# One list-scheduled order over all engines for a conditioned sliding-window attention and gMLP block

## Chip, cores, metric

The kernel runs on one core of a Trainium2 chip, written instruction by instruction in Bass. The metric is device time in microseconds (us), the median of several executions. A run counts as slow when it is over 1.5% above the fastest run of the same kernel; ratios use the other runs alone. Engines are called PE (TensorE matmul), PEld (its weight load), DVE (VectorE), ACT (ScalarE), POOL (GpSimd) and SP (SyncE, which here only issues DMAs).

## The reference, cut to what matters

```python
S, D, H, Dh, W = 2048, 448, 16, 28, 256        # tokens, width, heads, head width, window
mod = silu(c) @ w_mod                          # six vectors of 448: sa, ca, ga, sb, cb, gb
h = layernorm(x) * (1 + ca) + sa
q, k, v = split(h @ wqkv)                      # 16 heads of 28
p = softmax(where(0 <= i - j < 256, q @ k.T * 28**-0.5, -1e9))
x = x + ga * ((p @ v) @ wo)
h = layernorm(x) * (1 + cb) + sb
z = gelu(h @ w_in)                             # 2048 x 1792
z1, z2 = z[:, :896], layernorm(z[:, 896:])
g = w_sp @ z2 + b_sp                           # spatial matmul, 2048 x 2048 times 2048 x 896
x = x + gb * ((z1 * g) @ w_out)
```

Tokens are worked in 16 tiles of 128. With the window of 256 a tile of queries sees at most three tiles of keys, so attention is 128 "units" (16 tiles times 8 pairs of heads). A unit is six small score products, one exponential over 128 x 768, a mask, and six small products of probabilities with V ("PV").

## The kernel before

The author fixes the order on every engine by the order of the Python calls. The stages follow one another: loads, LayerNorm and QKV of all four blocks of 512 tokens, attention, z2 and z1, spatial matmul and output. Only the projections of the tile before are woven into attention, at fixed units.

```python
    ln1_dve(0) ... ln1_dve(3)
    transp_block(0)
    for tb in range(NB4):                       # QKV of all four blocks
        if tb + 1 < NB4:
            transp_block(tb + 1)
        qkv_block(tb)
        ...
    all_qk = [QKT_ready[k] for k in QKT_ready]  # every score waits for all of QKV
    # ... cut ...
    LAG = 3
    for u in range(LAG, NU + LAG):              # attention: one unit a step
        if u < NU:
            issue_S(u)                          # six score products
            issue_exp_mask(u)                   # ACT exp, DVE multiply with the mask
        issue_PV(u - LAG)
        # ... cut ...
        if tprev >= 0:                          # the tile before, at fixed units
            if ui == 1:   c1(tprev)             # PE transposes o, DVE copies it back
            elif ui == 3: c3(tprev, ...)        # projection with wo, residual
            elif ui == 4: c5(tprev)             # LayerNorm statistics
            elif ui == 7: c6(tprev, ...)        # PE transposes, DVE modulates
```

After attention, the second gate is multiplied into `w_out` on POOL, and the z2 tiles begin:

```python
    t_wout_g = sc.op("pool", lambda e: e.tensor_tensor(
        w_out_g[:], w_out_g[:], gg_sb[:, 1:2, :].broadcast_to([128, 7, D]), ALU.mult), [t_wout, t_gg])
    # ... cut: z2_tile: 8 matmuls, gelu to f32, statistics, normalisation to bf16
```

The softmax here doesn't subtract the row's maximum and nothing guards it: scores larger than these inputs give would overflow.

Of the kernel before, what the change touches and what calls it, by code (L numbers as in the profile page):

```python
# [8 lines left out]
ENGS = ("pe", "act", "dve", "pool", "sp")  # L9


class _Sched:

    def __init__(self, sems):
        self.sems = sems
        self.prog = {e: [] for e in ENGS}
        self.cnt = {e: 0 for e in ENGS}
        self.waited = {e: {} for e in ENGS}
        self.dma_cnt = {}

    def wait(self, eng, tk):
        if tk is None:
            return
        key, val = tk
        if self.waited[eng].get(key, 0) >= val:
            return
        self.waited[eng][key] = val
        self.prog[eng].append(("wait", key, val))

    def op(self, eng, fn, waits=(), sig=True):  # L30
        for w in waits:
            self.waitany(eng, w)
        if sig:
            self.cnt[eng] += 1
            self.prog[eng].append(("op", fn, eng, 1))
            return (eng, self.cnt[eng])
        self.prog[eng].append(("op", fn, None, 0))
        return None

    def waitany(self, eng, w):  # L40
        if w is None:
            return
        if isinstance(w, list):
            for t in w:
                self.waitany(eng, t)
            return
        self.wait(eng, w)

    def dma(self, fn, sem, waits=(), eng="sp"):
        for w in waits:  # L50
            self.waitany(eng, w)
        self.dma_cnt[sem] = self.dma_cnt.get(sem, 0) + 16
        self.prog[eng].append(("op", fn, ("dma", sem), 16))
        return (("dma", sem), self.dma_cnt[sem])

    def emit(self, eng, e):
        for item in self.prog[eng]:
            if item[0] == "wait":
                _, key, val = item
                sem = self.sems[key] if isinstance(key, str) else key[1]  # L60
                e.wait_ge(sem, val)
            else:
                _, fn, key, inc = item
                inst = fn(e)
                if key is not None:
                    sem = self.sems[key] if isinstance(key, str) else key[1]
                    inst.then_inc(sem, inc)


def bass_adaLN_cond__sliding_block__mixer_gmlp__prompt_kernel(  # L70
# [16 lines left out]
    DC = 4  # L87
    CH = 112
    NB4 = NT // 4
# [3 lines left out]
    ARENA_BYTES = 207 * 1024  # L93
    arena = nc.alloc_sbuf_tensor("arena", [128, ARENA_BYTES // 2], BF16)
    base = nc.lookup_mloc(arena).addr
    cursor = [0]

    def alloc(name, shape, dt, at=None):
        size = 1
        for s_ in shape[1:]:  # L100
            size *= s_
        nbytes = (size * mybir.dt.size(dt) + 31) // 32 * 32
        if at is None:
            off = cursor[0]
            cursor[0] += nbytes
        else:
            off = at
        assert off + nbytes <= ARENA_BYTES, (name, off, nbytes)
        return nc.alloc_sbuf_tensor_at(name, list(shape), dt, offset=base + off), off, nbytes

    x_sb, x_off, _ = alloc("x_sb", [128, NT, D], BF16)
    x1 = x_sb
    hT, _, _ = alloc("hT", [CH, DC, S], BF16)
    w_spT, _, _ = alloc("w_spT", [128, NT, S], BF16)
    bsp_bc, _, _ = alloc("bsp_bc", [128, S], BF16)
    modT_sb, _, _ = alloc("modT_sb", [128, 16], F32)
    ident, _, _ = alloc("ident", [128, 128], BF16)
    st_all, _, _ = alloc("st_all", [128, 3, NT, 2, 6], F32)
    mv_all, _, _ = alloc("mv_all", [128, 3, NT, 2], F32)
    ve_all, _, _ = alloc("ve_all", [128, 3, NT], F32)  # L120
    rs_all, _, _ = alloc("rs_all", [128, 3, NT], F32)
    neghalf, _, _ = alloc("neghalf", [128, NT], F32)
    rec_all, _, _ = alloc("rec_all", [128, NT, H], F32)
    mask01, _, _ = alloc("mask01", [128, 2, 128], BF16)
    phase_base = cursor[0]
    xn_all, _, _ = alloc("xn_all", [128, NT, D], BF16)
    wqkv_st, _, _ = alloc("wqkv_st", [CH, DC, 3 * D], BF16)
    WQK, _, _ = alloc("WQK", [CH, DC, 32, 32], BF16)
    wo_g, _, _ = alloc("wo_g", [CH, DC, D], BF16)
    gg_sb, _, _ = alloc("gg_sb", [128, 2, D], F32)  # L130
    sc_sb, _, _ = alloc("sc_sb", [CH, DC], BF16)
    cT_sb, _, _ = alloc("cT_sb", [CH, DC], BF16)
    Vaug, _, _ = alloc("Vaug", [128, NT, H, 32], BF16)
    oT_sb, ot_off, _ = alloc("oT_sb", [CH, 2, DC, 128], BF16)
    o_sb, _, _ = alloc("o_sb", [128, 3, D], BF16)
    NPT = 6
    PT, pt_off, _ = alloc("PT", [128, NPT, 6, 128], BF16)
    xn2, xn2_off, _ = alloc("xn2", [128, 3, D], BF16)
    sc_rep, _, _ = alloc("sc_rep", [CH, DC, 128], BF16, at=xn2_off + 1152)
    identf, _, _ = alloc("identf", [128, 128], F32, at=xn2_off + 2176)  # L140
    qkt_off = cursor[0]
    QKT, _, _ = alloc("QKT", [128, 8, S], BF16)
    abc_end = cursor[0]
    wmodA_sb, _, _ = alloc("wmodA_sb", [CH, DC, 2 * D], BF16, at=qkt_off)
    wmodB_sb, _, _ = alloc("wmodB_sb", [CH, DC, 4 * D], BF16, at=ot_off)
    assert ot_off + DC * 4 * D * 2 <= xn2_off + 1152

    def wm(v):
        return (wmodA_sb, v * D) if v < 2 else (wmodB_sb, (v - 2) * D)
    cursor[0] = phase_base  # L150
    w_in_sb, _, _ = alloc("w_in_sb", [CH, DC, 2 * FH], BF16)
    w_out_g, _, _ = alloc("w_out_g", [128, 7, D], BF16)
    assert cursor[0] <= phase_base + NT * D * 2 + DC * 3 * D * 2
    z2, _, _ = alloc("z2", [128, NT, FH], BF16)
    z1T, _, _ = alloc("z1T", [128, 7, S], BF16)
    z2raw, _, _ = alloc("z2raw", [128, 2, FH], F32)
    tmpg, _, _ = alloc("tmpg", [128, 2, 512], BF16)
    fin, _, _ = alloc("fin", [128, 4, D], BF16)
    d_end = cursor[0]
    assert max(abc_end, d_end) <= ARENA_BYTES, (abc_end, d_end)  # L160

    ps = nc.alloc_psum_tensor("ps", [128, 8, 512], F32)

    sem_names = ["pe", "act", "dve", "pool", "sp"]
    dma_sem_names = ["d_c", "d_wmodA", "d_wmodB", "d_x0", "d_x1", "d_x2", "d_x3", "d_wqkv", "d_wo",
                     "d_win", "d_wout", "d_bsp", "d_wsp0", "d_wsp1", "d_o0", "d_o1", "d_o2", "d_o3"]
    sem_handles = {}
    sem_ctx = []
    for n in sem_names + dma_sem_names:
        cm = nc.semaphore(n)  # L170
        sem_ctx.append(cm)
        sem_handles[n] = cm.__enter__()
    sc = _Sched({k: sem_handles[k] for k in sem_names})
    DS = {k: sem_handles[k] for k in dma_sem_names}
# [3 lines left out]
    wqkv_d = A_wqkv.rearrange("(c p) n -> p c n", p=CH)  # L178
    wo_d = A_wo.rearrange("(c p) n -> p c n", p=CH)
    win_d = B_w_in.rearrange("(c p) n -> p c n", p=CH)  # L180
    wout_d = B_w_out.rearrange("(f p) n -> p f n", p=128)
    wmod_d = w_mod.rearrange("(c p) n -> p c n", p=CH)
    cT_d = c[0].rearrange("(c p) -> p c", p=CH)
    bsp_d = B_b_sp[:].partition_broadcast(128)

    def _dma_c(e):
        with nc.allow_non_contiguous_dma(reason="tiny transposed load of c"):
            return e.dma_start(cT_sb[:], cT_d)
    t_x = [None] * 4
    t_x[0] = sc.dma(lambda e: e.dma_start(x_sb[:, 0:4, :], x_d[:, 0:4, :]), DS["d_x0"])  # L190
    t_c = sc.dma(_dma_c, DS["d_c"])
    t_wmodA = sc.dma(lambda e: e.dma_start(wmodA_sb[:], wmod_d[:, :, 0:2 * D]), DS["d_wmodA"], eng="act")
    t_wqkv = sc.dma(lambda e: e.dma_start(wqkv_st[:], wqkv_d), DS["d_wqkv"])
    for i in range(1, 4):
        t_x[i] = sc.dma(lambda e, i=i: e.dma_start(x_sb[:, 4 * i:4 * i + 4, :], x_d[:, 4 * i:4 * i + 4, :]), DS["d_x%d" % i])
    t_wmodB = sc.dma(lambda e: e.dma_start(wmodB_sb[:], wmod_d[:, :, 2 * D:6 * D]), DS["d_wmodB"], eng="act")
    t_wo = sc.dma(lambda e: e.dma_start(wo_g[:], wo_d), DS["d_wo"])
    t_bsp = sc.dma(lambda e: e.dma_start(bsp_bc[:], bsp_d), DS["d_bsp"])
    for tk in [t_c, t_wmodA, t_wqkv, t_wmodB, t_wo, t_bsp] + t_x:
        sc.wait("sp", tk)  # L200
    t_wspT = []
    for si in range(NT):
        sem = DS["d_wsp%d" % (si % 2)]
        tk = sc.dma(lambda e, si=si: e.dma_start_transpose(out=w_spT[:, si, :], in_=B_w_sp[:, si * 128:(si + 1) * 128]), sem)
        sc.wait("sp", tk)
        t_wspT.append(tk)
# [19 lines left out]

    bank_free = {b: [] for b in range(8)}
    MODV = (0, 1, 3, 4)
    last = None
    t_modT_pe = {}  # L230
    def modT_mm(vis, bank):
        nonlocal last
# [114 lines left out]
    for tb in range(NB4):  # L347
        if tb + 1 < NB4:
            transp_block(tb + 1)
# [368 lines left out]
```

## Time and profile before

| | before |
|---|---|
| median of the first three runs | 435.22 us (432.95 to 438.85) |
| profiled span | 436.2 us |
| PE busy | 359.3 us (82%) |
| DVE busy | 220.0 us (50%) |
| mean granted PE clock | 0.797 |

A window table gives, for each stretch of time, its length and the busy time of PE, PEld, DVE, ACT and POOL in us with instruction counts in brackets; then the granted PE clock (1.00 is full speed), the DMA share, and GB/s. The stretches here are the stages of the kernel before: start, QKV, attention, z2/z1, spatial matmul and output.

```profile
0.00:42.00 42.00, 18.71 (x111) 11.16 (x112) 20.48 (x59) 11.84 (x18) 8.57 (x18) 0.98 0.82 198
42.00:84.00 42.00, 40.26 (x222) 19.50 (x220) 9.40 (x16) 21.10 (x35) 3.60 (x1) 0.89 0.57 129
84.00:238.00 154.00, 125.58 (x1612) 74.97 (x1612) 113.86 (x304) 91.93 (x128) 9.77 (x17) 0.51 0.10 24
238.00:313.00 75.00, 56.97 (x256) 25.70 (x257) 46.87 (x97) 30.74 (x44) 15.53 (x19) 0.88 0.00 1
313.00:436.00 123.00, 117.73 (x551) 54.69 (x559) 29.35 (x44) 0.64 (x2) 32.29 (x28) 1.00 0.05 16
```

Attention takes 154 of 436 us, with no engine full (PE 82%, DVE 74%, ACT 60%, POOL 6%) and the clock at half. The spatial matmul, by contrast, is PE at 96% and full clock. There is little to win there.

Two parts of the page agree. The first line is the chain that ended last, by engine; the others are groups (busy us, mean ns of one, and the idle time before them with its main releaser).

```profile
PE 29%; DVE 26%; issue 24%; POOL 12%; ACT 5%; DMA 3%; POOLq 0%; SPq 0%; DVEq 0%
...
L412 ACT ACTIVATE PT<-ps 128x768 bf16<-128x768 f32 (+2 forms) x128 | 92.2, 771 | 61.7 <-PE ps L401 61.4
...
L419 DVE TENSOR_TENSOR PT<-PT,mask_61 128x512 bf16<-128x512 bf16 x112 | 44.8, 421 | 18.1 <-ACT PT L412 18.1
...
L476 PE MATMUL ps<-wo_g,oT_sb 112*128 112x448 bf16 x64 | 26.5, 570 | 4.0 <-DVE oT_sb L466 4.0
```

The chain is shared between PE and DVE, the mark of two engines handing work to and fro. The masks alone are 44.8 us of DVE. The projection's matmuls take 570 ns each at the granted clock of 0.51 of this stage, where the same width takes 352 ns at 1.00 (the output matmuls of the last stage). The waits of PE (us in total, times, longest):

```profile
PE ps L497 <- DVE xn_73 L488: 23.8, 16, 7.5
PE ps L240 <- ACT sc_sb L224: 15.6, 1, 15.6
PE ps L443 <- DVE o_sb L451: 12.8, 15, 1.4
```

L497 is the transpose of the normalised tile, L443 the first PV product of a tile. Both wait once per tile on something in DVE's in-order queue. The 15.6 us are the conditioning vector at the start. The longest wait, 7.5 us, lies where attention ends. The timeline shows it (start, duration, what, and in brackets the idle time before it):

```profile
238.18 6.15 POOL L539 TENSOR_TENSOR w_out_g<-w_out_g,gg_sb 128x3136 bf16<-128x3136 bf16 x1
238.25 6.21 DVE L488 TENSOR_SCALAR xn_73<-x_sb,mv_all,rs_all 128x448 bf16<-128x448 bf16 x1 [0.65 <-POOL rs_all L276]
```

A normalisation that otherwise takes 0.40 us (395 ns at the least, 396 at the median of the sixteen) takes 6.21 us beside a POOL multiply of 6.15 us, and the two end within 0.2 us of each other (244.33 and 244.46 us). So much the trace shows; that the one held up the other is the author's reading.

### The profile page before, as it was taken

Reading aid. Unit: us, or ns where it says so; the run is one execution under the profiler, and the core shown is the slowest. Engines: PE = TensorE matmul, PEld = TensorE weight load, DVE = VectorE, ACT = ScalarE, POOL = GpSimd, SP = SyncE. Lnnn points to the kernel's source line nnn. Section 1 sums busy time; section 2 is a strip of 40 time slices with the busy share of each in tenths; the row PEclk is TensorE's granted clock in tenths of the full one; section 3 lists DMA queues with packets and bytes.
Section 4 is the critical chain, followed back from the end, with each engine's and each line's share of the span. In section 5 each row is a group of like instructions: output and inputs, shape, how many; then the busy total and the mean of one; then the engine's idle time right before and its main releaser. Section 6 shows DMA issues by size and latency. Waiting matters only on the chain.

```text
span 436.2 us, 6559 instructions
## 1 busy us (share of the span) xinstructions
PE 359.3 (82%) x2749; PEld 186.0 (43%) x2760; DVE 220.0 (50%) x519; ACT 156.3 (36%) x224; POOL 69.8 (16%) x82
## 2 busy tenths in 40 slices
PE   0278999977888888888785567888999999999995
PEld 0243544444555544555453223333444444444442
DVE  0477122467777777777777767775012312313212
ACT  1063464756566655666653222447500000000000
POOL 4010300000000020000002411111033233233231
PEclk9998699955555555555555588999999999999999
DMA  8966646730000043000000000000000100100001
GB/s 211 297 169 102 143 99 145 123 71 2 2 2 2 2 127 97 2 2 2 2 0 2 0 1 2 1 2 0 0 2 0 44 0 0 44 0 11 32 0 44
DMA packets 40638, 19.44 MB, mean 45 GB/s; under 512 B 34176, under 2 KB 39184, under 8 KB 40608
## 3 DMA queue, kind: packets, MB, share of 16 engines
q1 hardware_dynamic: 39232, 14.19, 14.0%
q10 hardware_dynamic: 928, 2.41, 2.1%
q0 software_dynamic: 448, 2.41, 1.9%
q8 instruction: 22, 0.36, 0.4%
q14 instruction: 8, 0.07, 0.0%
HBM read 8.78 MB, written 1.84 MB: 24 GB/s over the span
## 4 chain that ended last, share of the span: by engine, by line
PE 29%; DVE 26%; issue 24%; POOL 12%; ACT 5%; DMA 3%; POOLq 0%; SPq 0%; DVEq 0%
DVE st_all L270 7%; POOL z1T L634 7%; PE ps L401 6%; PE ps L476 6%; POOL rs_all L276 5%; DVE PT L419 5%; PE ps L315 4%; PE ps L443 4%; ACT PT L412 3%; DMA cT_sb<-in_c_dram 3%; DVE xn_73 L488 3%; PE ps L328 3%; DVE z_81 L566 2%; DVE o_sb L451 2%; DVE mv_all L272 2%
## 5 line engine op out<-in xcount | busy, mean ns | idle before, releaser
L412 ACT ACTIVATE PT<-ps 128x768 bf16<-128x768 f32 (+2 forms) x128 | 92.2, 771 | 61.7 <-PE ps L401 61.4
L627 PE MATMUL ps<-w_spT,z_81 128*128 128x512 bf16 x437 | 96.4, 379 | 0.6
L627 PEld LDWEIGHTS ps<-w_spT,z_81 128*128 128x128 bf16 x448 | 43.9, 98 | 52.6
L631 DVE TENSOR_TENSOR tmpg<-ps,bsp_bc 128x512 bf16<-128x512 f32 x28 | 19.4, 692 | 88.7 <-PE ps L627 88.7
L276 POOL TENSOR_TENSOR rs_all<-ve_all,neghalf 128x1 f32<-128x1 f32 (+1 forms) x36 | 21.4, 595 | 251.6 <-DVE ve_all L275 251.6
L401 PE MATMUL ps<-QKT 32*128 32x128 bf16 x720 | 60.4, 297 | 0.9 <-ACT PT L412 0.7
L419 DVE TENSOR_TENSOR PT<-PT,mask_61 128x512 bf16<-128x512 bf16 x112 | 44.8, 421 | 18.1 <-ACT PT L412 18.1
L443 PE MATMUL ps<-Vaug,PT 128*128 128x32 bf16 x720 | 41.5, 190 | 13.6 <-DVE o_sb L451 12.8
L634 POOL TENSOR_TENSOR z1T<-tmpg,z1T 128x512 bf16<-128x512 bf16 x28 | 32.3, 1153 | 93.5 <-DVE tmpg L631 93.5
L443 PEld LDWEIGHTS ps<-Vaug,PT 128*128 128x128 bf16 x720 | 28.8, 105 | 37.8 <-DVE o_sb L451 16.3
L401 PEld LDWEIGHTS ps<-QKT 32*128 32x128 bf16 x720 | 28.3, 118 | 19.6 <-issue 11.3
L556 PE MATMUL ps<-w_in_sb,hT 112*128 112x448 bf16 x128 | 30.4, 394 | 3.2 <-ACT z2raw L560 3.2
L315 PE MATMUL ps<-hT,WQK 112*128 112x512 bf16 x128 | 29.7, 389 | 1.1 <-ACT QKT L318 1.1
L497 PE MATMUL ps<-ident,xn_73 128*112 128x128 bf16 x64 | 10.8, 324 | 23.8 <-DVE xn_73 L488 23.8
L476 PE MATMUL ps<-wo_g,oT_sb 112*128 112x448 bf16 x64 | 26.5, 570 | 4.0 <-DVE oT_sb L466 4.0
L560 ACT ACTIVATE z2raw<-ps 128x896 f32<-128x896 f32 x16 | 14.7, 917 | 34.1 <-DVE z_81 L566 15.8
L580 PE MATMUL ps<-hT,w_in_sb 112*128 112x512 bf16 x112 | 25.7, 379 | 1.3 <-ACT z1T L583 1.3
L331 DVE CAST Vaug<-ps 128x448 bf16<-128x448 f32 x16 | 9.9, 623 | 28.0 <-PE ps L328 27.3
L647 PE MATMUL ps<-w_out_g,z1T 128*128 128x448 bf16 x112 | 21.8, 352 | 2.1 <-POOL z1T L634 2.1
L318 ACT ACTIVATE QKT<-ps 128x512 bf16<-128x512 f32 x32 | 19.0, 599 | 11.2 <-PE ps L315 11.1
L556 PEld LDWEIGHTS ps<-w_in_sb,hT 112*128 112x128 bf16 x128 | 13.3, 109 | 19.8 <-ACT z2raw L560 6.6
L503 DVE TENSOR_SCALAR hT<-ps,modT_sb 112x128 bf16<-112x128 f32 x64 | 21.7, 401 | 0.0
(61 smaller groups left out, 299.2 us busy)
## 6 DMA issues: line engine op xcount, KB each, us to landing
x_sb<-in_A_x_dram SPq DMA_DIRECT2D x4, 448.0 KB, 15.5
out_dram<-fin SPq DMA_DIRECT2D x16, 112.0 KB, 2.1
wmodB_sb<-in_w_mod_dram ACTq DMA_DIRECT2D x1, 1568.0 KB, 13.7
w_in_sb<-in_B_w_in_dram POOLq DMA_DIRECT2D x1, 1568.0 KB, 8.9
wqkv_st<-in_A_wqkv_dram SPq DMA_DIRECT2D x1, 1176.0 KB, 17.1
wmodA_sb<-in_w_mod_dram ACTq DMA_DIRECT2D x1, 784.0 KB, 7.3
w_out_g<-in_B_w_out_dram POOLq DMA_DIRECT2D x1, 784.0 KB, 11.0
bsp_bc<-in_B_b_sp_dram SPq DMA_DIRECT2D x1, 512.0 KB, 9.5
```

What stands on the lines that cost most here:

```text
L270: tks.append(sc.op("dve", lambda e, t=t, ci=ci, s_ap=s_ap: e.bn_stats(st_all[:, slot, t, ci, :], s_ap), src_waits(t)))
L276: t_rs = sc.op("pool", lambda e: e.tensor_tensor(rs_all[:, slot, t0:t1], ve_all[:, slot, t0:t1], neghalf[:, t0:t1], ALU.pow), [t_ve, t_nh])
L315: last = sc.op("pe", lambda e, g=g, kc=kc, bank=bank: e.matmul(ps[:, bank, :], lhsT=WQK[:, kc, 4 * g:4 * g + 4, :].rearrange("p a b -> p ( ...
L401: last = sc.op("pe", lambda e, hh=hh, kb=kb, bank=bank, bi=bi, hg=hg, j=j: e.matmul(ps[:, bank, bi * 128:(bi + 1) * 128], lhsT=QKT[32 * hh ...
L412: t_exp = sc.op("act", lambda e: e.activation(PT[:, pb, :, :].rearrange("p (h b) q -> p h b q", b=3)[:, :, 0:nb, :], ps[:, 2 * sb:2 * sb + ...
L419: t_m = sc.op("dve", lambda e: e.tensor_tensor(ptv[:, :, 0:3:2, :], ptv[:, :, 0:3:2, :], mask01[:].unsqueeze(1).broadcast_to([128, 2, 2, 1 ...
L443: last = sc.op("pe", lambda e, slot=slot, kb=kb, h=h, bi=bi, nb=nb: e.matmul(ps[:, 4, 32 * h:32 * h + 32], lhsT=PT[:, pb, slot, :], rhs=Va ...
L476: last = sc.op("pe", lambda e, cc=cc, tb2=tb2: e.matmul(ps[:, 6, 0:D], lhsT=oT_sb[:, tb2, cc, :], rhs=wo_g[:, cc, :], start=(cc == 0), sto ...
L556: last = sc.op("pe", lambda e, t=t, hf=hf, kc=kc, banks=banks: e.matmul(ps[:, banks[hf], 0:D], lhsT=hT[:, kc, t * 128:(t + 1) * 128], rhs= ...
L580: last = sc.op("pe", lambda e, ft=ft, tb=tb, kc=kc, bank=bank: e.matmul(ps[:, bank, :], lhsT=w_in_sb[:, kc, ft * 128:(ft + 1) * 128], rhs= ...
L627: last = sc.op("pe", lambda e, si=si, ft=ft, tb=tb, bank=bank: e.matmul(ps[:, bank, :], lhsT=z2[:, si, ft * 128:(ft + 1) * 128], rhs=w_spT ...
L634: t_u = sc.op("pool", lambda e, mb=mb, ft=ft, tb=tb: e.tensor_tensor(z1T[:, ft, tb * 512:(tb + 1) * 512], tmpg[:, mb, :], z1T[:, ft, tb * ...
```

## The change

The whole kernel is rebuilt around a small planner. Each operation is declared with its dependencies, its buffer, a priority, and a modelled cost on each engine that could run it. A list scheduler picks, engine by engine, the operation that can start first (ties by priority) and so fixes one order for all five engines. Stages now overlap: block 0's attention can start when block 0's QKV is there, and QKV of blocks 1 to 3 is mixed into it. Loads are issued in the order in which they are needed. Beside that, work moves:

- masks leave DVE for two POOL selects of 256 columns per unit;
- both per-tile PE transposes become DMA transposes issued by SP, on the same queue as the 32 transposes of the spatial weight;
- the second LayerNorm's scale and shift are folded into `w_in` (scale on the rows, shift as a bias row), and the gates' products move to DVE;
- the gelu products leave POOL for DVE, and the z2 buffer becomes bf16.

```diff
-    all_qk = [QKT_ready[k] for k in QKT_ready]
-                w = (S_free[sb] + all_qk) if first else []
+            deps = [QK_op[(hg, j // 4)]] + [QK_op[(4 + hg, kb // 4)] for kb in kbs]
+            s_op = P.op("S%d_%d" % (j, ui), pr, [("pe", 36 * 2 * nb, s_fn)], deps, alloc=ten)
 ...
-            t_m = sc.op("dve", lambda e: e.tensor_tensor(
-                ptv[:, :, 0:3:2, :], ptv[:, :, 0:3:2, :], mask01[:]...broadcast_to([128, 2, 2, 128]), ALU.mult), ...)
+            k_op = P.op("M%d_%d" % (j, ui), pr, [("pool", (2 if nb == 3 else 1) * pool_ns(256), m_pool)],
+                        [e_op] + t_mask, uses=[pt])
 ...
-    c1: four PE transposes of o_sb into PSUM, one DVE copy to oT_sb
+        t1 = P.op("oT%d" % j, pr, [("sp", 100, lambda e, ...: e.dma_start_transpose(
+            out=oT[:, oTt.slot, :, :], in_=o_sb[:, ot.slot, :]))], [nrm, t_opad], alloc=oTt,
+            table="tr", dma=(131072, 2000), uses=[ot])
 ...
+    for n, si in enumerate([6, 7, 8, 9, 10, 11, 0, 1, 2, 3, 4, 5, 12, 13, 14, 15]):
+        for hf in range(2):                     # the spatial weight, 32 transposes, also on SP
+            wsp_op[(si, hf)] = P.op("wsp%d_%d" % (si, hf), 50 + n, [("sp", 100, fn)], deps,
+                                    table="wsp", dma=(300000, 1500))
 ...
+    P.predicted = P.schedule()
+    P.emit(handles, dma_sems)
```

Lines of the diff that name `c1` in words stand for code that was cut.

## The prediction

> **What bounds the kernel now.** The window table gives four stages. Until 42 us it waits for data: the conditioning vector lands at 15.2 us (chain of waits). QKV runs 42 to 84 us. Attention runs to 238 us, 10.14 us per token tile of eight two-head units. The MLP's z2/z1 run to 313 us: 6 us are lost to a Pool multiply of 6.15 us that also stretched a VectorE normalisation to 6.21 us (timeline), then 2.97 us per z2 tile, set by VectorE's statistics chain. The spatial matmul and output end at 436 us at clock 1.00: 28 groups of 3.45 us, four output blocks of 5.3 us.

> In attention no engine is full: per 20 us, PE 16.4, VectorE 14.9, ACT 11.9 us busy. Good stretches run one unit per 0.705 us (score bank round trip: scores 0.50 + exp 0.81 us + hand-offs, two bank pairs). Eight would take 5.7 us; the other 4.4 us are PE waiting on in-order VectorE work (1.45 and 1.0 us), two PE transposes, and the gated projection at 1.65 us. The granted clock is 0.50. [...] continuous scores and PV from 90 to 96 us did not open it.

> **What the change does.**
> - Loads in needed order: QKV of block 0 can start near 13 us instead of 29, attention near 17 to 20 us instead of 84.
> - QKV of blocks 1 to 3 goes inside attention. It is not removed: PE still pays 10 us (warm) to 20 us (cold) a block.
> - Both per-tile PE transposes (2 x 0.65 us) and their evacuations (0.68 + 1.36 us of VectorE) become DMA transposes; the LayerNorm modulation is folded into the input weights.
> - Masks leave VectorE (0.42 us) for two Pool selects of 256 columns. The trace has 128 columns at 0.29 us; I estimate 0.4 us, so 0.8 us per unit, about 105 us of Pool in all: nearly full, not the limit.
> - The z2 buffer becomes bf16; gelu products leave Pool (1.15 us) for VectorE; tail about 4 us shorter.

> Two-head score units are not new: no gain. The spatial matmul's PE work is unchanged.

> **Critical path afterwards: PE.** From 13 us on, QKV, attention units (118 full equivalents), projections and small products cost, with durations from the trace, an estimated 132 us at full clock and 207 us at half. Mixed with QKV I expect the clock partly open, half in the last six tiles: about 175 us with stalls, so attention ends near 186 us. z1/z2 becomes PE-bound: about 50 us instead of 75. Spatial matmul and output: about 119 us.

> 186 + 50 + 119 = 355 us; range 322 to 390. Faster by over 2%: 0.97; within 2%: 0.02; slower: 0.01.

> **What would show it.** Window table: first exp before 22 us; last exp at 165 to 210 us; spatial matmul starting at 220 to 260 us; VectorE below 60% in attention; Pool selects near 0.4 us; clock above 0.5 while QKV is mixed in. Waits: PE seldom waiting on masks.

> **What would make it wrong.** PE is in order and places each projection by a modelled latency; if the DMA transposes land late behind the 32 spatial-weight transposes on the same queue, PE stops once per tile (380+). Selects at 0.6 us would make Pool the limit. A clock open through attention gives about 320.

A clause on what opens the clock is cut from this text, since no run of this case had shown it. No term of the sum is cut: 186 + 50 + 119 = 355 us. The 10 us a block of QKV are the 40.26 us of PE in 42 to 84 us over four blocks, and 20 is twice that; they, the Pool selects of 0.6 us and the 320 us with an open clock are estimates.

## The result

| | before | after |
|---|---|---|
| median of four runs | 434.39 us (432.95 to 438.85) | 365.68 us (363.75 to 367.79) |
| ratio of the fast runs | 1 | 0.8398 (95% interval 0.8336 to 0.8459) |
| profiled span | 436.2 us | 362.0 us |
| PE busy | 359.3 us (82%) | 326.0 us (90%) |
| DVE busy | 220.0 us | 171.7 us |
| POOL busy | 69.8 us | 117.4 us |
| mean granted PE clock | 0.797 | 0.891 |

A ratio is the mean time of one kernel's fast runs over that of the other's of the same rounds on the same chip, so not quite the ratio of the medians quoted. Experiments ran on several chips; each has the kernel before beside it, so the ratios are what is compared. In e1_spread one run of four, in e4_dummy and e7_costs two of four counted as slow: they are in the medians and ranges quoted, not in the ratios.

The window table after, by the new stages (wait, first QKV, mixed and pure attention, z2/z1, spatial matmul and output):

```profile
0.00:16.00 16.00, 5.25 (x49) 4.00 (x50) 7.38 (x28) 3.28 (x6) 5.80 (x19) 1.00 0.86 256
16.00:44.00 28.00, 27.38 (x185) 10.17 (x186) 19.09 (x46) 16.39 (x31) 8.29 (x18) 1.00 0.58 180
44.00:190.00 146.00, 126.05 (x1589) 63.99 (x1599) 71.09 (x155) 89.66 (x117) 93.28 (x239) 0.73 0.51 83
190.00:240.00 50.00, 49.71 (x251) 23.89 (x255) 33.67 (x92) 30.18 (x43) 10.08 (x18) 0.99 0.04 9
240.00:362.00 122.00, 117.60 (x552) 54.60 (x559) 40.46 (x72) 0.61 (x2) 0.00 (x0) 1.00 0.05 16
```

Of the 74 us between the two spans (the medians differ by 69), 48 come from the time until attention ends (238 to 190), 25 from z2/z1 (75 to 50), and 1 from the last stage. DVE, which was at 74% in attention, is at 49% (71.09 of 146). The z stage is PE at 99%, which is what the kernel before lacked. The page's lines for the chain and the groups:

```profile
PE 80%; DMA 7%; SPq 4%; ACT 3%; DVE 3%; issue 2%; POOL 0%; DVEq 0%; ACTq 0%
...
L629 ACT ACTIVATE PT<-ps 128x768 bf16<-128x768 f32 (+2 forms) x128 | 93.8, 770 | 55.3 <-PE ps L427 54.3
...
L640 POOL TENSOR_SCALAR_AFFINE_SELECT PT<-PT 128x256 bf16<-128x256 bf16 x128 | 52.8, 414 | 21.3 <-ACT PT L629 21.2
...
L427 PE MATMUL ps<-wo_sb,oT 128*128 128x448 bf16 x64 | 23.2, 473 | 10.5 <-DMA oT<-o_sb 10.5
```

The chain is now 80% PE. What is left of it beside PE is mostly DMA (7%) and SP's queue (4%), and the last line tells where: 10.5 us in which PE stood before a projection, for the transposed attention output. The waits of PE say how often:

```profile
PE ps L427 <- DMA oT<-o_sb: 10.5, 5, 4.3
PE ps L427 <- ACT sc_sb L420: 10.2, 1, 10.2
PE ps L427 <- ACT PT L629: 5.2, 15, 0.5
PE ps L427 <- POOL PT L640: 2.0, 4, 0.9
```

The waits on DVE, 23.8 and 12.8 us before, are gone. POOL's masks hold PE up for 2.0 us in all. The timeline of SP's queue shows the cause of the five stops, followed by PE's longest stop from PE's own timeline:

```profile
41.18 17.81 SPq L728 DMA_TRANSPOSE w_spA<-in_B_w_sp_dram  x12
59.04 1.26 SPq L671 DMA_TRANSPOSE oT<-o_sb  x1
60.35 1.26 SPq L689 DMA_TRANSPOSE hT<-xn_80  x1
61.71 17.69 SPq L728 DMA_TRANSPOSE w_spA<-in_B_w_sp_dram  x12
79.44 1.26 SPq L671 DMA_TRANSPOSE oT<-o_sb  x1
```

```profile
82.19 1.76 PE L427 MATMUL ps<-wo_sb,oT 128*128 128x448 bf16 x4 [4.31 <-DMA oT<-o_sb]
```

A transpose of the spatial weight keeps the queue 1.48 us (17.81 over 12), not the planner's 0.1. Twelve in a row block the queue for 18 us, and the transposes that attention needs stand behind them. Finally the clock, in finer windows of the same kernel:

```profile
50.00:60.00 10.00, 9.98 (x121) 5.00 (x120) 4.47 (x9) 4.43 (x6) 4.59 (x13) 0.83 1.06 174
60.00:70.00 10.00, 7.43 (x114) 4.08 (x114) 7.30 (x16) 6.75 (x9) 6.39 (x15) 1.00 0.88 162
70.00:80.00 10.00, 6.66 (x85) 3.42 (x81) 5.66 (x11) 4.79 (x6) 7.14 (x18) 0.56 1.06 178
80.00:90.00 10.00, 7.45 (x56) 2.61 (x58) 3.92 (x8) 2.86 (x4) 1.95 (x6) 0.50 0.29 60
...
100.00:130.00 30.00, 29.17 (x376) 15.01 (x379) 19.92 (x41) 19.97 (x26) 19.92 (x52) 1.00 0.22 28
130.00:140.00 10.00, 8.13 (x128) 4.73 (x128) 3.95 (x9) 8.68 (x12) 9.44 (x26) 0.80 0.58 86
140.00:190.00 50.00, 41.61 (x563) 22.20 (x564) 16.32 (x41) 34.01 (x44) 34.95 (x94) 0.50 0.42 64
```

While QKV is mixed in, the clock is mostly full; in the last 50 us, attention alone, it is at half. Between lies a cold hole at 70 to 90 us. The stop at 78 to 82 us lies in it but did not begin it: by the trace's record of the clock, it closed at 71.23 us and opened again at 91.71 us.

### The profile page after: what moved, and what is told of

It reads as the page before. It is cut to its first block, busy times and chain, and to the rows that moved or that the text cites. A ratio compares the mean times of both kernels' runs of the same rounds, so it can differ in the third digit from the quotient of the medians.

```text
span 362.0 us, 6545 instructions
## 1 busy us (share of the span) xinstructions
PE 326.0 (90%) x2620; PEld 156.6 (43%) x2648; DVE 171.7 (47%) x390; ACT 140.1 (39%) x197; POOL 117.4 (32%) x294
## 3 DMA queue, kind: packets, MB, share of 16 engines
HBM read 8.78 MB, written 1.84 MB: 29 GB/s over the span
## 4 chain that ended last, share of the span: by engine, by line
PE 80%; DMA 7%; SPq 4%; ACT 3%; DVE 3%; issue 2%; POOL 0%; DVEq 0%; ACTq 0%
PE ps L427 80%; DMA oT<-o_sb 5%; SPq L728 4%; ACT PT L629 3%; DMA cT_sb<-in_c_dram 2%; DVE w_out_sb L716 1%; DVE st_all L490 1%; DVE hT L534 0%; ACT L419 0%; DVE fin L820 0%; DVE WQK L542 0%; POOL rs_all L486 0%; DVE x_sb L682 0%; DVE sc_rep L421 0%; DVEq L829 0%
## 5 line engine op out<-in xcount | busy, mean ns | idle before, releaser
L427 PE MATMUL ps<-w_spA,z_73 128*128 128x512 bf16 x329 | 76.6, 379 | 0.4
L638 POOL TENSOR_SCALAR_AFFINE_SELECT PT<-PT 128x256 bf16<-128x256 bf16 x112 | 46.5, 415 | 52.9 <-ACT PT L629 51.9
L640 POOL TENSOR_SCALAR_AFFINE_SELECT PT<-PT 128x256 bf16<-128x256 bf16 x128 | 52.8, 414 | 21.3 <-ACT PT L629 21.2
L427 PEld LDWEIGHTS ps<-w_spA,z_73 128*128 128x128 bf16 x336 | 32.8, 98 | 39.6
L427 PE MATMUL ps<-hT,WQK 128*128 128x512 bf16 (+1 forms) x115 | 39.1, 412 | 1.5 <-ACT PT L629 0.4
L427 PE MATMUL ps<-Vaug,PT 128*128 128x29 bf16 x720 | 34.3, 183 | 2.3 <-POOL PT L640 1.9
L427 PE MATMUL ps<-wo_sb,oT 128*128 128x448 bf16 x64 | 23.2, 473 | 10.5 <-DMA oT<-o_sb 10.5
L427 PE MATMUL ps<-w_spB,z_73 128*128 128x512 bf16 x109 | 28.3, 379 | 0.2
L427 PE MATMUL ps<-w_in_sb,hT 128*128 128x448 bf16 (+1 forms) x128 | 26.8, 356 | 0.0
L427 PE MATMUL ps<-hT,w_in_sb 128*128 128x512 bf16 (+1 forms) x107 | 25.5, 379 | 0.3
L427 PE MATMUL ps<-w_out_sb,z1T 128*128 128x448 bf16 x112 | 21.8, 352 | 0.0
## 6 DMA issues: line engine op xcount, KB each, us to landing
w_out_sb<-in_B_w_out_dram SPq DMA_DIRECT2D x1, 784.0 KB, 12.8
bsp_bc<-in_B_b_sp_dram SPq DMA_DIRECT2D x1, 512.0 KB, 13.4
```

Source lines behind the costliest of these rows:

```text
L427: return e.matmul(out_, lhsT=lhsT, rhs=rhs, start=st, stop=sp, **kw)
L638: e.affine_select(out=v[:, :, 0, :], in_=v[:, :, 0, :], pattern=[[0, 2], [-1, 128]], compare_op=ALU.is_gt, fill=0.0, base=0, channel_multi ...
L640: return e.affine_select(out=v[:, :, nb - 1, :], in_=v[:, :, nb - 1, :], pattern=[[0, 2], [1, 128]], compare_op=ALU.is_ge, fill=0.0, base= ...
```

## The experiments

Twelve kernels were run. All outputs are right. Where two theories are set against each other, the text says what each expected.

### Weight transposes two at a time (e1_spread)

Only SP's order changes: two of the spatial weight's transposes follow each `h2T` transpose.

```diff
     P.predicted = P.schedule()
+    wl = [o for o in P.order if o.name.startswith("wsp")]
+    new = []
+    for o in P.order:
+        if o in wl: continue
+        new.append(o)
+        if o.name.startswith("h2T"):
+            new += wl[:2]
+            del wl[:2]
+    P.order = new
```

> The changed kernel with the orders of PE, VectorE, ACT and Pool untouched; only the DMA-issuing queue differs: the 32 spatial-weight transposes go two after each token tile's second transpose instead of in blocks of 12, 12 and 8. Theory A (the blocks, 17.8 us for 12, hold back the small transposes, and PE, in order, stops at the output projections): PE's waits on the attention-output transpose fall from 10.5 us to under 3 us, the half-clock stretch from 71 to 91 us mostly goes, attention ends 8 to 18 us earlier than 190 us, total 347 to 358 us, ratio to before 0.80 to 0.825. Theory B (those waits only stand in place of other waits on exp and masks): under 3 us gained, ratio 0.832 to 0.845.

Measured: 362.0 us (358.64 to 364.81), ratio 0.8301 (0.824 to 0.8362), against 0.8398 for the changed kernel. The intervals overlap, so by itself this is not a proven gain. PE's waits on the transposed output fell from 10.5 us to 3.5 us, yet the last exponential started only 2.5 us earlier (185.2 instead of 187.7 us). SP's queue, then PE, show the largest stop that was left:

```profile
86.50 3.40 SPq L728 DMA_TRANSPOSE w_spA<-in_B_w_sp_dram  x2
89.94 1.26 SPq L671 DMA_TRANSPOSE oT<-o_sb  x1
```

```profile
92.75 1.36 PE L427 MATMUL ps<-wo_sb,oT 128*128 128x448 bf16 x4 [2.09 <-DMA oT<-o_sb]
```

Even two weight transposes (3.40 us) come at the wrong moment, and PE stops for 2.09 us. The granted clock was 1.00 in 80 to 90 us, 0.66 in 90 to 100 us, and 0.50 in 100 to 110 us, though PE was busy 10.00 of 10 us there. So the mixed work after this stop ran at half clock. Dispersing the transposes was the wrong remedy, and this run suggested the next one.

### Weight transposes after everything (e6_late)

Again only SP's order changes. All 32 are issued after the last `h2T`; they then have the z stage to land in.

```diff
+    wl = [o for o in P.order if o.name.startswith("wsp")]
+    wl.sort(key=lambda o: o.name.endswith("_1"))          # first halves first
+    rest = [o for o in P.order if o not in wl]
+    k = max(i for i, o in enumerate(rest) if o.name.startswith("h2T")) + 1
+    P.order = rest[:k] + wl + rest[k:]
```

> The changed kernel, PE, VectorE, ACT and Pool orders untouched; all 32 spatial-weight transposes come after the last small transpose of the queue, first the halves that the first output blocks need. Theory A (a stop of PE of 2 to 5 us at an output projection also shuts the clock gate, and the mixed stretch then runs at half clock for 15 to 20 us; so taking away the stops is worth several times their own length): PE's waits on the attention-output transpose under 2 us in all, clock 1.00 from 75 to 130 us, attention ends at 170 to 180 us, total 347 to 357 us, ratio 0.80 to 0.82. Theory B (the clock falls in the mixed stretch for other reasons, as it did in e1_spread although the waits fell to 3.5 us): total 359 to 364 us, like e1_spread.

Measured: 350.73 us (346.62 to 351.36), ratio 0.8047 (0.799 to 0.8105). That is 0.035 below the changed kernel, some 15 us of 435, with every other engine's order untouched. PE's waits on the transposed output fell to 0.2 us in all, the last exponential started at 174.3 instead of 187.7 us, and the spatial matmul at 226.6 instead of 239.9 us. The windows of this run:

```profile
60.00:70.00 10.00, 10.00 (x98) 4.41 (x96) 5.54 (x12) 4.94 (x8) 5.33 (x13) 0.50 0.08 15
...
80.00:120.00 40.00, 38.70 (x485) 19.50 (x492) 27.37 (x57) 26.11 (x34) 27.26 (x71) 1.00 0.17 31
...
130.00:174.00 44.00, 39.50 (x556) 21.57 (x552) 16.27 (x41) 33.37 (x45) 34.84 (x94) 0.50 0.20 38
```

The stops had cost 10.3 us directly, of the 13.4 us by which the last exponential came earlier. The clock opened earlier than in the changed kernel (78.24 instead of 91.71 us), but it had also closed earlier, at 54.35 us: between 20 and 125 us it was closed for 23.9 us in both profiles, and in the tail for 6.8 us less here. So in this pair of profiles the stops themselves are most of the gain. Theory A's total held (347 to 357 us), but not its reason, that stops are worth several times their own length. One profile is only one sample of the clock: over the four runs of e6_late its mean ranges from 0.896 to 0.915, which with their spans makes an estimated 59 to 72 us of closed clock. The cold hole at 60 to 70 us is there without any long stop, so it has another cause (e4 and e9 below).

### A planner with measured durations (e7_costs)

The planner's figures for scores, PV, selects, projection and transposes are replaced by durations near those measured (a small transpose 100 to 1260 ns, a weight transpose 100 to 1300 ns), and the weight transposes are made to depend on all `h2T`.

```diff
-            s_op = P.op(..., [("pe", 36 * 2 * nb, s_fn)], ...)
+            s_op = P.op(..., [("pe", 72 * 2 * nb, s_fn)], ...)
-        [("sp", 100, lambda e, ot=ot, ...: e.dma_start_transpose(
+        [("sp", 1260, lambda e, ot=ot, ...: e.dma_start_transpose(
 ... the others likewise
```

> As e6_late, but through the scheduler: it is told the durations measured here (432 ns for six score matmuls instead of 216, 264 for six PV instead of 156, 373 for a projection matmul instead of 190, 405 for a Pool select, 1260 ns of queue time for a small transpose instead of 100), and the weight transposes depend on the last small one. Theory A (the list order is close to what the chip does, and its errors of a factor of two do not matter, since in-order waits are few): within 4 us of e6_late. Theory B (the wrong durations are what sets PE's order wrong): 8 us or more faster than e6_late.

Measured: 352.95 us (349.27 to 356.05), ratio 0.8056 (0.7998 to 0.8114), not told apart from e6_late. Better durations alone brought nothing beyond the order on SP's queue. The loss was that one queue, not the planner's estimates in general.

### Attention only after all of QKV (e2_serial, e5_serial_ev)

Both undo the overlap: every score waits for all of QKV, as in the kernel before. Everything else stays, with the transposes dispersed as in e1_spread, which is the run to compare with. In e2_serial the evacuations of QKV blocks 2 and 3 are left to DVE alone, as in the change; e5_serial_ev lets ACT take its share (ACT is idle then).

```diff
-            deps = [QK_op[(hg, j // 4)]] + [QK_op[(4 + hg, kb // 4)] for kb in kbs]
+            deps = list(QK_op.values()) + list(V_op.values())
-    EVB = 1
+    EVB = 3                                   # e5_serial_ev only
```

> As e1_spread, but every score unit waits for the QKV projection of all four token blocks, so that QKV and attention don't overlap, as in the kernel before. Theory A (PE's own work is the limit, and QKV does not vanish by being overlapped): QKV runs at clock 1.00 to about 60 us, attention at clock 0.50 and about 1.0 us per full unit as in the last six tiles of the changed kernel, so it ends at 172 to 190 us; total within 12 us of e1_spread. Theory B (the gain comes from overlapping the stages): attention ends about 30 us later than in e1_spread, total 380 us or more.

Measured: 389.86 us (387.39 to 390.23), ratio 0.8956 (0.8907 to 0.9005). The first exponential started at 88.6 us, the last at 210.8 us. But PE waited on DVE between 46 and 61 us (3.05 and 2.31 us at the longest), so part of this loss came of the experiment itself. Hence the second:

> e2_serial again (no overlap of QKV and attention), but ACT and VectorE may share the evacuation of all four QKV blocks, because in e2_serial blocks 2 and 3 were evacuated by VectorE alone and QKV lasted to 88 us. Theory A (without that handicap the serial order costs little, because PE's work is the same): QKV done by 62 to 72 us, attention again near 1.03 us per full unit and about 122 us long, total 364 to 374 us, within 12 us of e1_spread. Theory B (overlap itself is worth over 20 us, since serial attention runs all at half clock while mixed attention runs partly at full clock): total 380 us or more.

Measured: 385.39 us (384.13 to 386.61), ratio 0.8859 (0.8807 to 0.8911), 0.056 or some 24 us above e1_spread. QKV now ended near 84 us with PE nearly full, and still:

```profile
85.00:211.00 126.00, 107.42 (x1471) 58.91 (x1471) 38.27 (x100) 93.59 (x130) 94.42 (x252) 0.51 0.52 86
```

This is the whole of attention at half clock, PE at 85%. So the overlap is worth about 24 us. Pure attention, even with masks and transposes moved off, did not fill PE or open its clock here; mixed with dense QKV products it mostly did both. It also shows what the rest of the rebuild is worth without the overlap: 385.39 against 435.73 us.

### Masks back on VectorE (e3_dvemask)

The masks go back to DVE as one multiply per unit. Since the planner sees this, the whole order shifts a little. Compare with the changed kernel.

```diff
-            k_op = P.op(..., [("pool", (2 if nb == 3 else 1) * pool_ns(256), m_pool)], ...)
+            k_op = P.op(..., [("dve", 421 if nb == 3 else 292, m_dve)], ...)
```

> The changed kernel with the masks as one VectorE multiply per unit (0.42 us) instead of two Pool selects (0.41 us each); the scheduler is told 421 ns. Theory A (the mask's engine is off the limit; PE and the transposes set the pace): total within 6 us of 365.7 us, VectorE 7 to 9 us busy per 10 us where QKV is mixed in. Theory B (freeing VectorE of the masks is a main source of the gain, because of its in-order queue): attention ends 15 us or more later, total 380 us or more.

Measured: 382.97 us (382.31 to 383.31), ratio 0.8809 (0.876 to 0.8859), 0.041 or some 18 us above the changed kernel. PE's waits on the exponential grew from 5.2 us in 15 places to 15.5 us in 34, and the last exponential started at 205.7 us:

```profile
PE ps L427 <- ACT PT L629: 15.5, 34, 1.0
```

DVE did not become full (123.5 of 186 us in 20 to 206 us). In 50 to 130 us PE was as busy as in the changed kernel (70.4 of 80 us in both), but at a clock of 0.67 instead of 0.85, so there the loss is clock. My reading is that masks in DVE's in-order queue hold up the evacuations of QKV and so spread its products out (the last came at 161.6 instead of 132.9 us). It is not shown: the planner's new order may do the same, and no run separated the two.

### Dummy products in attention's tail (e4_dummy)

Where attention runs alone, useless dense products of 128 x 384 are put ahead of each unit's scores, into banks that the scores then overwrite: one per unit in tiles 10 to 12, two in tiles 13 to 15.

```diff
+                for r in range(0 if j < 10 else 1 if j < 13 else 2):
+                    mm(e, ps[:, ten.slot + r, 0:384], QKT[:, 0, 0:128], QKT[:, 4, 0:384], True, True)
```

> The changed kernel with throw-away matmuls of 128 rows and 384 columns into the score banks just before the scores overwrite them: one per unit in token tiles 10 to 12, two in tiles 13 to 15; the result stays right. Theory A (the clock is half there because scores and PV are too thin to count as activity): the clock reads 1.00 in one or both stretches, projections take 0.8 instead of 1.75 us per tile, and the stretch from 134 us to the end of attention gets no longer or up to 5 us shorter although PE does more. Theory B (it is half because of gaps in PE's work, or for another reason): the clock stays 0.50 and the stretch gets about 0.32 us a unit longer in tiles 10 to 12 and 0.64 us in tiles 13 to 15, 20 us or more in all.

The 0.32 us are an estimate: 16 products of 512 columns take 3.45 us in the spatial matmul at a clock of 1.00; scaled to 384 columns and doubled for half clock, one takes 0.32 us.

Measured: 375.1 us (370.33 to 378.23), ratio 0.8561 (0.8483 to 0.8639), slower than the changed kernel. But the windows are the clearest:

```profile
160.00:170.00 10.00, 10.00 (x104) 4.18 (x103) 2.44 (x5) 6.17 (x8) 6.28 (x17) 0.50 0.14 28
170.00:180.00 10.00, 10.00 (x95) 3.59 (x90) 1.37 (x5) 5.67 (x7) 6.66 (x17) 0.50 0.14 27
180.00:190.00 10.00, 9.95 (x145) 4.80 (x144) 4.23 (x10) 6.80 (x9) 6.54 (x17) 0.95 0.15 30
190.00:200.00 10.00, 9.89 (x132) 5.15 (x128) 4.15 (x12) 8.30 (x11) 7.08 (x18) 1.00 0.14 28
```

With one dummy PE is busy all the time, 10.00 of 10 us, and the clock stays at 0.50. With two it opens, and the four projection matmuls fall from 1.76 to 1.03 us. So busy time alone did not open the clock here. The dummies cost more than the clock gave.

For e4_dummy this is an estimate, from its timeline with the columns spread over the times printed: with one dummy, some 2500 to 2970 in each step from 150.18 to 177.49 us; with two, some 3440 in the first step, still at half clock, and 3980 or more in the next ones. The count says what went together in these traces. It is not shown for the other kernels and was not tested by a run of its own.

### Transposes of the output back on PE (e8_peT)

On top of e6_late, the attention output is transposed by PE with a DVE copy, as before the change.

```diff
-        t1 = P.op("oT%d" % j, pr, [("sp", 100, lambda e, ...: e.dma_start_transpose(...
+        for kc in range(4):                   # PE transpose of 128 columns into a PSUM bank
+            tms.append(P.op("oTm%d_%d" % (j, kc), pr, [("pe", 60, tr_fn)], ...
+        t1 = P.op("oT%d" % j, pr, [("dve", 683, lambda e, ...: e.tensor_copy(oT..., ps...))], tms, ...)
```

> As e6_late, but the attention output is transposed on PE again (four matmuls with the identity and a 0.68 us VectorE copy per tile) instead of by DMA; one part of the change undone. Theory A (the DMA transpose saves PE work where PE is the limit, about 0.4 us per tile at half clock): 3 to 8 us slower than e6_late. Theory B (the 2.6 us from issue to landing and the queue cost PE more than its own transpose would): as fast or faster than e6_late.

The 0.4 us are an estimate: four products of 128 columns are as wide as one of 512, which takes 0.22 us in the spatial matmul and twice that at half clock.

Measured: 363.57 us (361.32 to 365.04), ratio 0.8358 (0.831 to 0.8407), 0.031 or some 13 us above e6_late. The last exponential started at 185.0 us. The clock was 0.50 at 70 to 90 us and 0.77 at 90 to 100 us, where e6_late had 1.00 from 80 us on. The DMA transpose is a gain, and more than theory A's 3 to 8 us, provided that its queue is free. The planner made a new order for this run, so part of the 13 us may be that order.

### The cold hole, the table load, and a longer mix (e9_preplate, e10_tab, e11_stretch)

In e6_late the clock closed at 54.35 us, right after 32 matmuls that stream one column each (the MLP's scale and shift, 50.11 us, 2.27 us of PE) and among the bias products, whose stationary operand is one column wide. The count under e4_dummy points to the former: in the changed kernel, too, the clock closed after the step with these 32. Three single changes on top of e6_late follow.

e9_preplate moves this preparation eight tiles later in priority:

```diff
-    m2, ten_m2 = mod_cols("modB", 3.0, (3, 4), t_wmB)
+    m2, ten_m2 = mod_cols("modB", 11.0, (3, 4), t_wmB)
 ... bias products, weight scalings and the second gate likewise, each + 8
```

> The late version with one thing more: the MLP's own preparation (shift and scale columns, the four bias products with a one-column stationary operand, the second gate and the weight scalings that hang on them) gets priorities eight tiles later, so it leaves the stretch where blocks 1 and 2 of QKV are mixed with attention. Theory A (those thin products let the clock gate close at 54 to 78 us of the late version): the granted clock in 50 to 80 us rises from 0.50-0.72 to 0.9 or more, the last exp starts 4 to 10 us earlier (164 to 170 us), and the ratio is 0.78 to 0.80 (341 to 348 us). Theory B (the gate closes there for another reason, for instance the transposes of block 2 or plain chance): the dip stays or moves, and the ratio stays at 0.80 to 0.815; the same few us of thin work now stand in the tail, where they are cold as well.

Measured: 350.76 us (347.76 to 352.9), ratio 0.8082 (0.8037 to 0.8126), no different from e6_late. Theory A was right about the hole: the clock was 1.00 from 20 to 110 us, for instance

```profile
60.00:70.00 10.00, 10.00 (x131) 5.30 (x131) 6.37 (x16) 6.52 (x10) 7.62 (x20) 1.00 0.14 28
```

It was wrong about the bias products, beside which the clock was open where they came later (114.1 to 120.0 us): all sixteen took 347 to 352 ns, where the median was 533 ns in e6_late. The time was theory B's. The last QKV product ended near 107 us instead of 125 us; from there attention was alone and cold, and as the moved one-column products came (the last at 109.7 us), the clock was at 0.83 in 110 to 120 us. The last exponential started at 171.6 us, only 2.7 us earlier.

e10_tab puts a one-element Silu ahead of the wait on the conditioning vector. In the changed kernel ScalarE's timeline shows the table load behind that wait:

```profile
8.41 1.28 ACT L419 ACT_TABLE_LOAD   x1 [8.41 <-DMA cT_sb<-in_c_dram]
```

```diff
+    t_tab = P.op("tab", -98, [("act", 180, lambda e: e.activation(tabx[:], ident[:, 0:1], ACT.Silu))], [t_ident], table="silu")
```

> The late version with a one-element Silu on the identity's first column ahead of the first wait on the conditioning vector, so that ScalarE's table load no longer stands behind that wait. Theory A (the load of 1.28 us lies on the chain to the first exp, and everything behind moves up with it): first mod column on PE 1 to 1.3 us earlier, the first exp starts near 23.5 instead of 24.8 us, and the time falls by 1 to 1.5 us (ratio 0.800 to 0.803). Theory B (something else of the start, the wqkv load or VectorE, is right behind it): the first exp moves by less than 0.5 us and the ratio is 0.803 to 0.807, not told apart from the late version's.

Measured: 350.46 us (349.35 to 351.95), ratio 0.8061 (0.802 to 0.8101), no gain. PE's first product started 1.4 us earlier (8.4 instead of 9.8 us), but the first exponential at 24.3 us, against 23.2 in e6_late's profile and 24.9 in e11_stretch's, neither of which has the early load. The traces show what took the rest. PE stood 0.61 us for DVE's LayerNorm statistics before the first transpose, and the clock opened at 20.15 us, against 16.80 in e6_late and 20.84 in e11_stretch. A second table load of 1.28 us, the exponential's, stands right before the first exponential in all three. No run took these apart.

e11_stretch lets QKV of blocks 2 and 3 come later, so that it lasts longer:

```diff
-        pr = 4 * tb - 2.5
+        pr = 4 * tb - (2.5 if tb < 2 else 1.2)
```

> The late version with QKV of blocks 2 and 3 at priorities 1.3 tiles later, so the dense products reach further into attention. Theory A (the clock is open as long as dense products are mixed in, and the tail of pure attention is cold): the clock stays open about one tile longer (to 135-140 us instead of 130), the cold tail has one tile less, the last exp starts 3 to 6 us earlier and the ratio is 0.79 to 0.80. Theory B (fewer dense products per tile are no longer enough, or attention units now wait for QKV of their own block): the clock drops in the mixed stretch or PE stops before tile 8 or 12, and the ratio is 0.805 or more.

Measured: 346.9 us (345.65 to 348.05), ratio 0.7976 (0.7939 to 0.8013), the best of all. Its interval meets that of e6_late and lies below those of e9 and e10 from the same rounds. The last QKV product ended near 131 us instead of 125 us, and the last exponential started at 169.5 us:

```profile
120.00:130.00 10.00, 10.00 (x137) 5.04 (x137) 5.56 (x12) 7.31 (x11) 7.60 (x20) 1.00 0.21 42
130.00:140.00 10.00, 8.89 (x148) 5.51 (x147) 3.65 (x9) 8.33 (x12) 8.13 (x23) 0.84 0.14 28
```

The same stock of dense products, taken out later, kept the clock open longer (0.84 in 130 to 140 us, where e6_late had 0.50).

### All together (e12_all)

The late transposes, the stretched QKV, the preparation 9.5 tiles later, and the early table load.

> All that has not hurt, together: late weight transposes, QKV of blocks 2 and 3 pushed back by 1.3 tiles, the MLP's preparation moved to tiles 12 to 14, and the early Silu table load. Theory A (what counts is how long attention runs with the clock open, and the dip of 54 to 78 us and the cold tail are two separate losses): the clock is 1.00 from 20 to 130 us without the dip, the last exp starts 2 to 6 us before the stretched version's 169.5 us, and the ratio is 0.780 to 0.793. Theory B (the dense products are a fixed stock: without the dip they are used up sooner, and the cold tail grows by as much as the dip gave): the clock falls to 0.50 about 10 us earlier than the stretched version's 138 us, and the ratio is 0.793 to 0.802, not told apart from the stretched version's.

Measured: 349.92 us (347.07 to 350.82), ratio 0.8044 (0.7992 to 0.8097), above e11_stretch in the mean, though the intervals just meet (0.7992 against 0.8013). So nothing was added, and something was probably lost. Theory B was right in its mechanism and too mild in its figures (ratio 0.793 to 0.802; the clock falling near 128 us). The clock was 1.00 to 110 us and then closed: 0.52 in 110 to 120 us, where the stretched version had 1.00 until 130 us. A priority only breaks ties in this planner, so with the preparation out of the way QKV filled the gap at once: its last product came near 107 us, as in e9. PE's timeline at the end of that stretch:

```profile
107.85 1.84 PE L429 MATMUL ps<-sc_sb,wmod_sb 64*128 64x1 bf16 x25
109.62 1.15 PE L429 MATMUL ps<-wo_sb,oT 128*128 128x448 bf16 x4
...
111.75 1.78 PE L429 MATMUL ps<-wmod_sb,sc_rep 128*128 128x448 bf16 x4
```

Four matmuls of 448 columns took 1.15 us just after the one-column products and 1.78 us two microseconds later. PE had not stopped between; the clock had closed. The step that ended there ran from 106.99 to 110.41 us, and the one-column products filled half of it (1.84 us). My estimate is that the end of QKV at 107 us would have closed the clock a little later: in e11_stretch, with no such products there, it closed at 136.90 us, after QKV's end near 131 us.

## Why the prediction was right

The range held: 365.68 us against 355, in 322 to 390. The sum was right stage by stage in the profile: attention's end 186 predicted and about 190 measured, z2/z1 50 and 50, spatial matmul and output 119 and 122.

- **PE as the limit afterwards: right.** The chain went from 29% to 80% PE. DVE in attention, predicted below 60%, was 49%.
- **The clock: right in direction, and worth about a third of the gain.** It was to be above 0.5 in the mix and half at the end; it was 1.00 in 100 to 130 us and 0.50 from 140 us, but also 0.50 to 0.56 in 70 to 90 us of the mix. e4_dummy shows that a busy PE alone was not enough: 10.00 of 10 us at 0.50 with one dummy, 9.95 at 0.95 with two. The prediction's own hint, continuous scores and PV that stayed cold in the kernel before, pointed the same way. With the overlap undone (e5_serial_ev) some 24 us are lost of the 74 us that e1_spread gains (1 less 0.8301, of 435.46 us); the other 50 are there without it.
- **POOL: right as to the limit, wrong as to its load.** Selects were estimated at 0.4 us and took 0.414 us; PE waited 2.0 us on them. But "nearly full" was wrong: POOL was busy 93.3 of 146 us, 64%. The prediction's own figures say as much: 105 us over the some 170 that it gave attention. What it did not price is what masks on DVE cost PE: e3_dvemask, with the planner's new order, puts their move at some 18 us.
- **The risk named was real and cost about 15 us.** "If the DMA transposes land late behind the 32 spatial-weight transposes on the same queue, PE stops once per tile." It stopped five times in sixteen tiles, 10.5 us in all. That was counted only as a risk. e6_late shows the whole cost, of which the stops are 10.3 us. The clock may have added to it: in e1_spread a stop of 2.09 us was followed by 17 us at half speed (93.20 to 110.26 us).
- **The start: wrong.** "QKV of block 0 can start near 13 us" and "first exp before 22 us". QKV began at 15.8 us and the first exponential at 24.8 us. The conditioning vector came at 8.4 us instead of 15.2, but the table load, the modulation columns, the transposes and their evacuation stand one behind another. PE was cold as well: the views print a clock of 1.00 before its first record (20.03 us), but at 18.08 us four products of 448 columns took 1.81 us, as long as at half clock (1.76). Shortening one link, e10_tab, moved PE's start and not the exponential's.
- **z2/z1: right in size.** There PE is 49.71 of 50 us busy; the normalisation of 6.21 us is gone, and a z2 normalisation takes 508 ns (bf16 input) instead of 746 ns (f32). This was read from the profiles; no run separated these parts.
- **The DMA transposes as a saving: right.** e8_peT, with the planner's new order, puts those of the output alone at some 13 us.

The difference between 355 and 366 has three small terms: attention's end 4 us later, the last stage 3 us longer, and 3.7 us by which the median lies above the profiled span (362.0; the time of that execution was 363.75 us). The "about 175 us with stalls" from 13 us on came out at about 177. It is right as a sum, and in part by luck. In the profile PE was busy 155.8 us of it, 63.0 at half clock, which makes some 124 us at full clock against the 132 predicted, and it stood still for 21.2 us. Part of it is the avoidable 15 us of the transposes' order: e11_stretch, without them and with the longer mix, takes 346.9 us.

## What to carry to other kernels

Before you give a queue of DMA transposes to a planner, measure how long each keeps the queue, and put long prefetches behind the short transfers that an in-order engine waits for. Look at the granted clock of each stretch, since a busy engine can be at half speed (e4_dummy: 10.00 of 10 us busy at 0.50). Where the clock goes with dense products, as it did here, treat them as a stock: mix them with the thin work for as long as possible (e11_stretch), and keep products that stream a single column out of the mix (the clock closed after them at 54.35 us of e6_late and 110.41 us of e12_all). When you take out one loss, look at what moves into its place before you add up gains: e9 removed the hole and e12 combined everything, and neither gained.

## Two more measurements from the traces

- A DMA transpose kept the queue that issues it 1.26 us for 128 x 512 and 1.48 us for 1024 x 128 of the spatial weight, so that twelve of the latter blocked the queue for 17.81 us. In 190 to 230 us of e6_late, where most of the 32 of the weight ran, the DMA engines were full (share 0.89 to 1.08) at 170 to 193 GB/s.
- The table load of ScalarE took 1.28 us, and the traces show no pause after it: in the changed kernel the load ran from 8.41 to 9.69 us and the Silu began at 9.71 us, and the exponential's load ran from 23.47 us, 0.02 us behind another activation, to 24.75 us, the exponential beginning at 24.76 us. The first load stood behind the wait of its activation there; in the kernel before it ran at 1.81 us, ahead of the wait.
